# One wide product for the high and low probabilities of attention, and an addition on the way out of PSUM

## The chip, the cores and the metric

The kernel runs on one core of a Trainium2 chip. The metric is the device time of one execution in microseconds. Three runs of the kernel before took 1193.26, 1195.87 and 1196.34 us; the median is 1195.87.

## The reference

Attention with two kinds of masks, and behind it a gated feed-forward layer over all tokens:

```python
# q, k, v: 8 batches, 8 heads, 576 positions, 64 wide, float32
rel = pos[:, None] - pos[None, :]
mask_plain = (rel >= 0) & (rel < 32)                     # heads 0 to 3
mask_dil = (rel >= 0) & (rel < 128) & (rel % 4 == 0)     # heads 4 to 7
scores = np.where(mask, q @ k.T / 8, -1e9)
attn = softmax(scores)                                   # exp(s - max) / (sum + 1e-9)
x = (attn @ v) as 4608 rows of 512
xn = x / sqrt(mean(x * x) + 1e-6) * rms_g
out = (silu(xn @ w_gate) * (xn @ w_val)) @ w_out         # 512 -> 1536 -> 512
```

## The kernel before, in words

**Tiling.** The 4608 rows are cut into 16 units of 288 (u = 0 to 15, half a sequence each). Everything of a unit stands transposed: features on partitions, the 288 rows in the free dimension. The 1536 hidden features are 12 pieces j of 128. Heads go in four pairs c; a pair's attention is cut into blocks: 3 blocks of 96 queries in the plain pairs c = 0 and 1, 4 blocks of 72 queries in the dilated pairs c = 2 and 3 (one for each residue class). So a unit has 14 blocks, 6 of nq = 96 and 8 of nq = 72.

**Precision.** Units 0 and 1 of the attention and unit 0 of the feed-forward layer (NNAT = 2) multiply in float32. All others split each operand in a high part, rounded to a shorter float (F32R), and a low part, the rest, and take three products: high by high, high by low and low by high (`three`, L543 to L545; L407 to L409 for the outputs of attention).

**Slots.** Python writes the order of all instructions out by hand, in slots. Three slots make one piece j: `gate` (12 products of 288 columns into PSUM tile g), `val` (12 into v) and `proj` of the piece before (12 into four tiles acc). A unit of the feed-forward layer is a stage of 36 slots. Behind the 12 products of a slot stand what the attention of the next unit has for it: at most one block's transposes (t, L394, into the free columns of g or v), one block's output products (o, L407 to L409, into the only tile o) and one block's score products (q, L420, into the only tile s). In a stage these blocks come every other slot; a block's outputs come 3 slots after its transposes and share their slot with the scores of a later block. The last about 9 slots of a stage have no outputs.

**What follows a product** on the other engines is put off to the start of the next slot (`later(1, rank, ...)`, `flush`), in the order of the ranks: 0 tanh of g (ACT) or the product with v (DVE, `prod`, L595); 0.2 `untranspose` (ACT copies the transposed probabilities as `pt`, L374, DVE takes the low part `pl`, L378); 0.5 `hhi` (ACT, L606, it waits for `prod`), then `take` (the block's outputs out of PSUM into `xraw`, L347); 0.7 `scores_max` (DVE, L307 and L312); 0.8 silu (DVE, L582). Exponentials, splits of q and k (L276, L281, L285, L290) and of the values (`vhi`, `vlo`, L247, L251) stand in later ranks. Each engine works its instructions off in that order. ACT is ScalarE, DVE VectorE, POOL GpSimd.

`pl` stands in the path of TensorE in one way that matters here: it reads the transposes out of the free columns of g or v, and the next `gate` or `val` starts that tile anew.

Of the kernel before, what the change touches and what calls it, by code (L numbers as in the profile page):

```python
# [9 lines left out]
F32 = mybir.dt.float32  # L10
BF16 = mybir.dt.bfloat16
F32R = mybir.dt.float32r
U32 = mybir.dt.uint32
AF = mybir.ActivationFunctionType
ALU = mybir.AluOpType
PSUM = bass.MemoryType.PSUM

B, H, S, D = 8, 8, 576, 64
DM, FF = 512, 1536
NT = B * S  # L20
P = 128
# [4 lines left out]
QB = 96  # L26
NC = DM // P
NJ = FF // P
NNAT = 2
# [15 lines left out]
def geometry(u, c):  # L45


    half = u % 2
    if c < NC // 2:
        if half:  # L50
            return [(QB * i, QB * i, 0, P) for i in range(U // QB)], QB, U + W
        return [(QB * i, max(QB * i - W, 0), 0 if i else W, P if i else QB)
                for i in range(U // QB)], QB, U
    nq = U // DIL
    keys = nq + (W if half else 0)
    return [(nq * r, keys * r, 0 if half else W, keys) for r in range(DIL)], nq, keys * DIL
# [3 lines left out]
def attn_moe(ctx: ExitStack, tc: tile.TileContext, qk_in, v_in, w_gate, w_val, w_out, rms_g, outT):  # L60
# [4 lines left out]
    V, A, G, PE = nc.vector, nc.scalar, nc.gpsimd, nc.tensor  # L65

    cst = ctx.enter_context(tc.tile_pool(name="cst", bufs=1))
    sb = ctx.enter_context(tc.tile_pool(name="sb", bufs=2))
# [29 lines left out]
    def later(dt, rank, fn):  # L98
        put_off.setdefault(now[0] + dt, []).append((rank, fn))
# [90 lines left out]
    heads, vs, late = {}, {}, []  # L190
# [32 lines left out]
    def load_v(b):  # L223

        if b is not None and b[0] >= NNAT:
            u, c, i = b
            vt = sb.tile([P, 2, D], F32, tag="vt", name=f"vt_{u}_{c}_{i}", bufs=3)
            nc.sync.dma_start(out=vt.rearrange("p a d -> p (a d)"), in_=v_in[u, c][:, i * 2 * D:(i + 1) * 2 * D])
            vs[b] = vt

    def further(b, n):

        k = everything.index(b) + n
        return everything[k] if k < len(everything) else None
# [6 lines left out]
    def split_v(b, dt):  # L241
        k = everything.index(b) % 2

        def hi():
            if k not in vparts:
                vparts[k] = [late[0].tile([P, 2, D], F32R, name=f"v{p}_{k}", bufs=1) for p in ("hi", "lo")]
            A.copy(out=vparts[k][0], in_=vs[b])  # L247

        def lo():
            vh, vl = vparts[k]  # L250
            G.tensor_tensor(out=vl, in0=vs.pop(b), in1=vh, op=ALU.subtract)  # L251
            load_v(further(b, 3))

        later(dt, 3.3, hi)
        later(dt, 5.1, lo)
# [42 lines left out]
    st, xraw, xsq = {}, {}, {}  # L298
# [18 lines left out]
    def scores_exp(u, c, i):  # L317
        blocks, nq, _ = geometry(u, c)
        n = blocks[i][3]
        t, sm = st[u, c, i]  # L320
        for a in range(2):
            A.activation(out=t[:nq, a, :n], in_=t[:nq, a, :n], func=AF.Exp, scale=-1.0,  # L322
                         bias=sm[:nq, a:a + 1], accum_out=sm[:nq, 2 + a:3 + a])
# [11 lines left out]
    def take(u, c, i, o):  # L335

        blocks, nq, _ = geometry(u, c)
        if (u, c) not in xraw:
            xraw[u, c] = sb.tile([P, U], F32, tag="xraw", name=f"xraw_{u}_{c}", bufs=NC)
        x = xraw[u, c]  # L340
        if c < NC // 2:
            to = x[:, QB * i:QB * i + nq]
        else:
            to = x.rearrange("p (j r) -> p r j", r=DIL)[:, i, :]
        copy = V.tensor_copy if i % 2 and u != 1 else A.copy
        for a in range(2):
            copy(out=to[a * D:(a + 1) * D], in_=o[a * D:(a + 1) * D, a * nq:(a + 1) * nq])  # L347
        if i == len(blocks) - 1:
            later(1, 2.5, lambda: square(u, c))

    def square(u, c):
        first = c == 0
        sq = sb.tile([P, U], F32, tag="xsq" if first else "tmp", name=f"sq_{u}_{c}", bufs=1 if first else 2)
        x = xraw[u, c]
        A.activation(out=sq, in_=x, func=AF.Square)
        if u == 0:
            G.tensor_scalar(out=x, in0=x, scalar1=gs[:, c:c + 1], scalar2=1.0, op0=ALU.mult, op1=ALU.mult)
        if first:
            xsq[u] = sq
        else:  # L360
            later(1, 0.4, lambda: (V if c == NC - 1 else G).tensor_tensor(out=xsq[u], in0=xsq[u], in1=sq, op=ALU.add))
# [6 lines left out]
    def untranspose(b, t_ps):  # L368
        blocks, nq, _ = geometry(*b[:2])
        n = blocks[b[2]][3]  # L370
        t_in = t_ps[:n].rearrange("k (a q) -> k a q", a=2)[:, :, :nq]
        exact = b[0] < NNAT
        pt = sb.tile([P, 2, QB], F32 if exact else F32R, tag="pt", name=f"pt_{b[0]}_{b[1]}_{b[2]}", bufs=2)
        A.copy(out=pt[:n, :, :nq], in_=t_in)  # L374
        st[b] = pt
        if not exact:
            pl = late[0].tile([P, 2, QB], F32R, tag="pl", name=f"pl_{b[0]}_{b[1]}_{b[2]}", bufs=2)
            V.tensor_tensor(out=pl[:n, :, :nq], in0=t_in, in1=pt[:n, :, :nq], op=ALU.subtract)  # L378
            st[b] = pt, pl

    def products(q, t, o, t_ps, s_tag="s", o_tag="o"):


        if q:
            s_ps = ps.tile([P, 512], F32, tag=s_tag, name=f"s_{q[0]}_{q[1]}_{q[2]}")
        if o:
            o_ps = ps.tile([P, 512], F32, tag=o_tag, name=f"o_{o[0]}_{o[1]}_{o[2]}")
            pt = st.pop(o)
        if t:
            p, _ = st.pop(t)  # L390
        def transposed(a):
            blocks, nq, _ = geometry(*t[:2])
            n = blocks[t[2]][3]
            PE.transpose(t_ps[:n, a * QB:a * QB + nq], p[:nq, a, :n], ident[:nq, :nq])  # L394

        def output(a):
            blocks, nq, _ = geometry(*o[:2])
            n = blocks[o[2]][3]
            if a:
                return  # L400
            out = o_ps[:, :2 * nq].rearrange("d (a q) -> d a q", a=2)
            if o[0] < NNAT:
                PE.matmul(out, vs.pop(o)[:n].rearrange("k a d -> k (a d)"), pt[:n, :, :nq], start=True, stop=True)
                return
            vh, vl = (part[:n].rearrange("k a d -> k (a d)") for part in vparts[everything.index(o) % 2])
            ph, pl = (part[:n, :, :nq] for part in pt)
            PE.matmul(out, vh, ph, start=True, stop=False)  # L407
            PE.matmul(out, vh, pl, start=False, stop=False)  # L408
            PE.matmul(out, vl, ph, start=False, stop=True)  # L409

        def scored(a):
            blocks, nq, _ = geometry(*q[:2])
            qc, kc, _, n = blocks[q[2]]
            sv = s_ps[:QB].rearrange("q (a t k) -> q a t k", a=2, t=2)
            if q[0] < NNAT:
                qr, kr = heads[q[0], 2 * q[1] + a]
                PE.matmul(sv[:nq, a, 0, :n], qr[:, qc:qc + nq], kr[:, kc:kc + n], start=True, stop=True)
                return
            qs, ks = heads[q[0], 2 * q[1] + a]
            PE.matmul(sv[:nq, a, :, :n], qs[:, qc:qc + nq], ks[:, :, kc:kc + n], start=True, stop=True)  # L420

        parts = [(b, fn, a) for b, fn in ((t, transposed), (o, output), (q, scored)) for a in range(2)]
        for b, fn, a in parts:
            if b:
                fn(a)
        if t:
            later(1, 0.2, lambda: untranspose(t, t_ps))
        if o:
            later(1, 0.5, lambda: take(*o, o_ps))
            if o[0] < NNAT:  # L430
                later(1, 9, lambda: load_v(further(o, 3)))
            far = further(o, 2)
            if far and far[0] >= NNAT:
                split_v(far, 8 if o[0] < NNAT else 1)
        if q:
            later(1, 0.7, lambda: scores_max(*q, s_ps))
            later(2, 2, lambda: scores_exp(*q))
            later(3 if q[0] < NNAT else 4, -1, lambda: scores_norm(*q))
            u, c, i = q
            nxt = after(u, 2 * c, 2)  # L440
            nb = len(geometry(u, c)[0])
            if u < NNAT:
                if u == NNAT - 1 and c == NC - 1 and i == nb - 1:
                    for a in range(2):
                        later(1, 9, lambda a=a: load(NNAT, a))
                        later(5 + a, 9, lambda a=a: split(NNAT, a, (1, 2, 2, 3), G, V))
            elif nxt and i == 0:
                split(*nxt, (1, 2, 2, 3), G, V)
                split(nxt[0], nxt[1] + 1, (2, 3, 3, 4), G, V)
# [224 lines left out]
    for n in range(ends):  # L674
# [8 lines left out]
        if n == ends - 1:  # L683
            _, v_free = gate(0, 0), val(0, 0)
# [3 lines left out]
    for u in range(NU):  # L688
        for j in range(NJ):
            for part in range(0 if u + j else 2, 3):  # L690
                t = 3 * (u * NJ + j) + part
# [94 lines left out]
```

## Time and profile before

| | |
|---|---|
| runs | 1193.26, 1195.87, 1196.34 us |
| profiled execution, its own time | 1192.86 us |
| its span, first to last instruction | 1190.7 us |
| granted TensorE clock over the span | 0.997 |
| TensorE busy with matmuls | 96% |
| VectorE, ScalarE, GpSimd busy | 63%, 57%, 54% |

Busy time is the union of an engine's instructions in the profile; the time of the profiled execution lies 2.2 us above its span, and 3.0 us below the median of the three runs. Starts in the timeline are in us from the start of the span. A matmul's recorded length (about 0.3 us) includes its way through the array and overlaps the next one, so what a product takes of TensorE is read from start to start.

### The profile page before, as it was taken

What the parts mean: (1) busy time and instruction counts of PE and PEld (TensorE: products, weight loads), DVE (VectorE), ACT (ScalarE), POOL (GpSimd) and SP (SyncE); (2) the same over time, 40 slices, a digit from 0 to 9 for tenths busy, and PEclk for the clock granted to TensorE, in tenths of its full rate; (3) what the DMA queues carried; (4) which work ended last, traced back from release to release, by engine and by line L of the source; (5) the groups of instructions that cost most, each with busy time, mean ns of one, the idle gap of its engine ahead of it and who ended that gap; (6) DMA issues with size and microseconds to landing.
All of it is one profiled execution on the core that took longest, in us unless ns stands there. A gap on an engine that the chain in (4) does not pass through costs nothing.

```text
span 1190.7 us, 26009 instructions
## 1 busy us (share of the span) xinstructions
PE 1140.4 (96%) x8492; PEld 1103.2 (93%) x8492; DVE 755.1 (63%) x2715; ACT 676.4 (57%) x2456; POOL 640.8 (54%) x1094
## 2 busy tenths in 40 slices
PE   4788899999999999999999999999999999999998
PEld 3566688999999999999999999999999999999998
DVE  4789786765658576665857656585765757575321
ACT  4567576564646556474656646465665646565221
POOL 2666476664646555464655655465555645565211
PEclk9999899999999999999999999999999999999999
DMA  4555321121213112121312212131221213120000
GB/s 151 188 186 188 106 82 50 58 80 32 77 38 92 45 51 80 35 81 36 90 40 70 68 30 78 38 101 38 68 61 35 81 37 93 40 77 16 1 21 20
DMA packets 62711, 82.19 MB, mean 69 GB/s; under 512 B 7442, under 2 KB 43282, under 8 KB 62578
## 3 DMA queue, kind: packets, MB, share of 16 engines
q1 hardware_dynamic: 61242, 79.60, 21.9%
q8 instruction: 68, 1.11, 0.4%
q10 hardware_dynamic: 1336, 0.94, 0.3%
q14 instruction: 65, 0.53, 0.1%
HBM read 71.08 MB, written 9.44 MB: 68 GB/s over the span
## 4 chain that ended last, share of the span: by engine, by line
PE 78%; DVE 14%; DMA 2%; ACT 2%; issue 2%; POOL 1%; SPq 0%; POOLq 0%; DVEq 0%
PE acc L543 8%; PE acc L544 7%; PE acc L545 7%; PE v L543 7%; PE g L543 7%; PE v L544 7%; PE v L545 7%; PE g L544 7%; PE g L545 7%; PE s L420 3%; DVE qs L290 3%; PE g L394 2%; PE o L408 2%; PE o L409 2%; DVE xraw L514 2%
## 5 line engine op out<-in xcount | busy, mean ns | idle before, releaser
L607 POOL TENSOR_TENSOR hlo<-th,hhi 128x288 fp32r<-128x288 f32 x180 | 145.4, 808 | 218.3 <-ACT hhi L606 214.2
L332 POOL TENSOR_SCALAR t<-t,sm 96x128 f32<-96x128 f32 (+3 forms) x448 | 185.2, 425 | 99.4 <-DVE sm L330 74.1
L543 PE MATMUL v<-xhi,hi_v 128*128 128x288 f32 x720 | 220.3, 306 | 3.5 <-DVE pl L378 3.2
L543 PE MATMUL acc<-hhi,hi_o 128*128 128x288 f32 x720 | 221.1, 307 | 0.0
L543 PE MATMUL g<-xhi,hi_g 128*128 128x288 f32 x720 | 219.8, 305 | 0.0
L544 PE MATMUL acc<-hlo,hi_o 128*128 128x288 f32 x720 | 212.8, 295 | 0.2 <-POOL hlo L607 0.2
L544 PE MATMUL g<-xlo,hi_g 128*128 128x288 f32 x720 | 212.9, 296 | 0.0
L544 PE MATMUL v<-xlo,hi_v 128*128 128x288 f32 x720 | 212.8, 296 | 0.0
L545 PE MATMUL acc<-hhi,lo_o 128*128 128x288 f32 x720 | 212.6, 295 | 0.0
L545 PE MATMUL g<-xhi,lo_g 128*128 128x288 f32 x720 | 212.6, 295 | 0.0
L545 PE MATMUL v<-xhi,lo_v 128*128 128x288 f32 x720 | 212.3, 295 | 0.0
L322 ACT ACTIVATE t<-t,sm 96x128 f32<-96x128 f32 (+3 forms) x448 | 166.7, 375 | 18.4 <-DMA k<-in_qk_dram 13.6
L251 POOL TENSOR_TENSOR vlo<-vt,vhi 128x128 fp32r<-128x128 f32 x196 | 98.5, 502 | 125.2 <-ACT vhi L247 109.3
L577 ACT ACTIVATE th<-g 128x288 f32<-128x288 f32 x180 | 74.0, 411 | 157.7 <-PE g L545 106.2
L606 ACT CAST hhi<-th 128x288 fp32r<-128x288 f32 x180 | 78.0, 433 | 141.2 <-DVE th L595 137.2
L543 PEld LDWEIGHTS v<-xhi,hi_v 128*128 128x128 f32 x720 | 135.3, 188 | 6.5 <-DVE pl L378 6.5
L307 DVE TENSOR_TENSOR t<-s,mask 96x256 f32<-96x256 f32 (+3 forms) x196 | 72.0, 367 | 106.7 <-PE s L420 101.1
L544 PEld LDWEIGHTS acc<-hlo,hi_o 128*128 128x128 f32 x720 | 135.8, 189 | 0.5 <-POOL hlo L607 0.5
L544 PEld LDWEIGHTS g<-xlo,hi_g 128*128 128x128 f32 x720 | 135.7, 188 | 0.1
L544 PEld LDWEIGHTS v<-xlo,hi_v 128*128 128x128 f32 x720 | 135.7, 188 | 0.0
L543 PEld LDWEIGHTS acc<-hhi,hi_o 128*128 128x128 f32 x720 | 135.5, 188 | 0.0
L543 PEld LDWEIGHTS g<-xhi,hi_g 128*128 128x128 f32 x720 | 135.3, 188 | 0.2 <-issue 0.2
(120 smaller groups left out, 2662.0 us busy)
## 6 DMA issues: line engine op xcount, KB each, us to landing
qk<-in_qk_dram SPq DMA_DIRECT2D x56, 288.0 KB, 2.9
vt<-in_v_dram SPq DMA_DIRECT2D x196, 64.0 KB, 1.8
qk<-in_qk_dram SPq DMA_DIRECT2D x28, 352.0 KB
out_dram<-ot SPq DMA_DIRECT2D x64, 144.0 KB, 1.9
qk<-in_qk_dram SPq DMA_DIRECT2D x28, 304.0 KB, 2.7
raw_g<-in_w_gate_dram SPq DMA_DIRECT2D x12, 512.0 KB, 3.1
raw_v<-in_w_val_dram SPq DMA_DIRECT2D x12, 512.0 KB, 4.0
raw_o<-in_w_out_dram SPq DMA_DIRECT2D x12, 512.0 KB
```

What stands on the lines that cost most here:

```text
L251: G.tensor_tensor(out=vl, in0=vs.pop(b), in1=vh, op=ALU.subtract)
L290: eq.tensor_tensor(out=qs[D:], in0=qr[D:], in1=qs[D:], op=ALU.subtract)
L307: V.tensor_tensor(out=t[:nq, :, :n], in0=sv[:nq, :, 1, :n], in1=mask[:nq, None, mc:mc + n].to_broadcast([nq, 2, n]), op=ALU.add)
L322: A.activation(out=t[:nq, a, :n], in_=t[:nq, a, :n], func=AF.Exp, scale=-1.0, bias=sm[:nq, a:a + 1], accum_out=sm[:nq, 2 + a:3 + a])
L332: G.tensor_scalar(out=t[:nq, a, :n], in0=t[:nq, a, :n], scalar1=sm[:nq, 2 + a:3 + a], scalar2=1.0, op0=ALU.mult, op1=ALU.mult)
L420: PE.matmul(sv[:nq, a, :, :n], qs[:, qc:qc + nq], ks[:, :, kc:kc + n], start=True, stop=True)
L543: PE.matmul(out, wh[:, cc, :], xh, start=start, stop=False)
L544: PE.matmul(out, wh[:, cc, :], xl, start=False, stop=False)
L545: PE.matmul(out, wl[:, cc, :], xh, start=False, stop=stop)
L577: A.activation(out=t, in_=g, func=AF.Tanh, scale=0.5)
L606: A.copy(out=hi, in_=t)
L607: G.tensor_tensor(out=lo, in0=t, in1=hi, op=ALU.subtract)
```

## The change

For the units from 2 on, the low part of the probabilities is no longer a tile of its own: `pt` gets a second half for it. The high part of the values is multiplied with both halves in one product of 4 nq columns, whose left half (2 nq columns) is high by high and whose right half is high by low. The third product, low values by high probabilities, is accumulated on the left half. So two products stand where three stood. The right half is added on the way out: `take` copies it to `xraw` on ACT (two instructions, one for each head of the pair), and then DVE adds the left half (two instructions). Before, `take` was two copies for each block, on DVE for odd i (block number in the pair) and on ACT for even i.

```diff
@@ take
-        for a in range(2):
-            copy(out=to[a * D:(a + 1) * D], in_=o[a * D:(a + 1) * D, a * nq:(a + 1) * nq])
+        if u < NNAT:
+            for a in range(2):
+                copy(out=to[a * D:(a + 1) * D], in_=o[a * D:(a + 1) * D, a * nq:(a + 1) * nq])
+        else:
+            for a in range(2):
+                A.copy(out=to[a * D:(a + 1) * D], in_=o[a * D:(a + 1) * D, (2 + a) * nq:(3 + a) * nq])
+            for a in range(2):
+                rows = slice(a * D, (a + 1) * D)
+                V.tensor_tensor(out=to[rows], in0=o[rows, a * nq:(a + 1) * nq], in1=to[rows], op=ALU.add)
@@ untranspose
-        pt = sb.tile([P, 2, QB], F32 if exact else F32R, tag="pt", ...)
-        A.copy(out=pt[:n, :, :nq], in_=t_in)
-        st[b] = pt
+        st[b] = pt = sb.tile([P, 2, 2, QB], F32 if exact else F32R, tag="pt", ...)
+        A.copy(out=pt[:n, 0, :, :nq], in_=t_in)
         if not exact:
-            pl = late[0].tile([P, 2, QB], F32R, tag="pl", ...)
-            V.tensor_tensor(out=pl[:n, :, :nq], in0=t_in, in1=pt[:n, :, :nq], op=ALU.subtract)
-            st[b] = pt, pl
+            V.tensor_tensor(out=pt[:n, 1, :, :nq], in0=t_in, in1=pt[:n, 0, :, :nq], op=ALU.subtract)
@@ products, output
-            ph, pl = (part[:n, :, :nq] for part in pt)
-            PE.matmul(out, vh, ph, start=True, stop=False)
-            PE.matmul(out, vh, pl, start=False, stop=False)
-            PE.matmul(out, vl, ph, start=False, stop=True)
+            both = o_ps[:, :4 * nq].rearrange("d (t a q) -> d t a q", t=2, a=2)
+            PE.matmul(both, vh, pt[:n, :, :, :nq], start=True, stop=False)
+            PE.matmul(out, vl, pt[:n, 0, :, :nq], start=False, stop=True)
```

In the changed kernel the lines stand elsewhere: L347 becomes L351 (ACT) and L354 (DVE), L378 becomes L383, L407 to L409 become L412 and L413, L420 becomes L424, L595 becomes L599, L606 becomes L610, L543 becomes L547.

**TensorE, at the end of a `val` slot**, with the outputs of block i = 1 of pair 0 and the scores of a later block. Names are tile, pair or head or piece, block, and a running number; the sizes are those of what is read and streamed. Before:

```order
L545 MATMUL v_0_7198<-xhi_3_7119,lo_v_674 128x288
L407 MATMUL o_0_1_7212<-pt_0_1_7111,vhi_1468 128x192
L408 MATMUL o_0_1_7212<-pl_0_1_7113,vhi_1468 128x192
L409 MATMUL o_0_1_7212<-pt_0_1_7111,vlo_1469 128x192
L420 MATMUL s_1_2_7211<-ks_2_6901,qs_2_6936 96x256
L420 MATMUL s_1_2_7211<-ks_3_6934,qs_3_6968 96x256
```

and now:

```order
L549 MATMUL v_0_7196<-xhi_3_7117,lo_v_674 128x288
L412 MATMUL o_0_1_7210<-pt_0_1_7110,vhi_1468 128x384
L413 MATMUL o_0_1_7210<-pt_0_1_7110,vlo_1469 128x192
L424 MATMUL s_1_2_7209<-ks_2_6901,qs_2_6936 96x256
L424 MATMUL s_1_2_7209<-ks_3_6934,qs_3_6968 96x256
```

One product is gone and one is twice as wide; no other row moves.

**VectorE in the slot after that**, from the product with v to the low part of the next transposes. Before:

```order
L595 TENSOR_TENSOR th_0_7186<-th_0_7186,v_0_7198 128x288 [waits DVE_49,PE_49]
L347 COPY xraw_0_7149<-o_0_1_7212 64x96 [waits PE_49]
L347 COPY xraw_0_7149<-o_0_1_7212 64x96
L307 TENSOR_TENSOR t_1_2_7225<-s_1_2_7211,mask 96x256 [waits PE_49]
L312 ISA t_1_2_7225,sm_1_2_7227<-s_1_2_7211,t_1_2_7225 96x128 [waits DVE_49]
L312 ISA sm_1_2_7227 96x1
L312 ISA t_1_2_7225,sm_1_2_7227<-s_1_2_7211,t_1_2_7225 96x128
L312 ISA sm_1_2_7227 96x1
L329 TENSOR_SCALAR sm_1_1_7154<-sm_1_1_7154 96x2 [waits Activation_49]
L330 RECIPROCAL sm_1_1_7154<-sm_1_1_7154 96x2 [waits DVE_49]
L378 TENSOR_TENSOR pl_1_0_7254<-v_0_7198,pt_1_0_7252 128x192 [waits Activation_49]
```

and now:

```order
L599 TENSOR_TENSOR th_0_7185<-th_0_7185,v_0_7196 128x288 [waits DVE_49,PE_49]
L354 TENSOR_TENSOR xraw_0_7146<-o_0_1_7210,xraw_0_7146 64x96 [waits PE_49,Activation_49]
L354 TENSOR_TENSOR xraw_0_7146<-o_0_1_7210,xraw_0_7146 64x96
L307 TENSOR_TENSOR t_1_2_7224<-s_1_2_7209,mask 96x256 [waits PE_49]
L312 ISA t_1_2_7224,sm_1_2_7226<-s_1_2_7209,t_1_2_7224 96x128 [waits DVE_49]
L312 ISA sm_1_2_7226 96x1
L312 ISA t_1_2_7224,sm_1_2_7226<-s_1_2_7209,t_1_2_7224 96x128
L312 ISA sm_1_2_7226 96x1
L329 TENSOR_SCALAR sm_1_1_7153<-sm_1_1_7153 96x2
L330 RECIPROCAL sm_1_1_7153<-sm_1_1_7153 96x2 [waits DVE_49]
L383 TENSOR_TENSOR pt_1_0_7251<-v_0_7196,pt_1_0_7251 128x192 [waits Activation_49]
```

The additions stand where the copies stood, and the first of them waits for ACT. The first addition waits for both copies of ACT: they give one signal, after the second.

**ScalarE in the same slot.** Before:

```order
L374 CAST pt_0_2_7188<-g_0_7167 128x192
L322 ACTIVATE t_1_1_7152,sm_1_1_7154<-t_1_1_7152,sm_1_1_7154 96x128 [waits DVE_49] x2
L606 CAST hhi_0_7219<-th_0_7186 128x288 [waits DVE_49]
L247 CAST vhi_1468<-vt_1_0_6816 128x128 [waits DMAHW6_49,PE_49]
L374 CAST pt_1_0_7252<-v_0_7198 128x192 [waits PE_49]
```

and now:

```order
L322 ACTIVATE t_1_1_7151,sm_1_1_7153<-t_1_1_7151,sm_1_1_7153 96x128 [waits DVE_49] x2
L610 CAST hhi_0_7216<-th_0_7185 128x288 [waits DVE_49]
L351 COPY xraw_0_7146<-o_0_1_7210 64x96 [waits PE_49]
L351 COPY xraw_0_7146<-o_0_1_7210 64x96
L247 CAST vhi_1468<-vt_1_0_6815 128x128 [waits DMAHW6_49]
L381 CAST pt_1_0_7251<-v_0_7196 128x192 [waits PE_49]
```

ACT's copies of the block stand behind `hhi`, which waits for `prod` on DVE. For even i they stood at this place of their slots before; there DVE now has the additions ahead of the scores.

More of the change, by code (lines that the diff above doesn't have):

```diff
@@ L372, in untranspose @@
         exact = b[0] < NNAT
-        pt = sb.tile([P, 2, QB], F32 if exact else F32R, tag="pt", name=f"pt_{b[0]}_{b[1]}_{b[2]}", bufs=2)
-        A.copy(out=pt[:n, :, :nq], in_=t_in)
-        st[b] = pt
+        st[b] = pt = sb.tile([P, 2, 2, QB], F32 if exact else F32R, tag="pt", name=f"pt_{b[0]}_{b[1]}_{b[2]}", bufs=2)
+        A.copy(out=pt[:n, 0, :, :nq], in_=t_in)
         if not exact:
-            pl = late[0].tile([P, 2, QB], F32R, tag="pl", name=f"pl_{b[0]}_{b[1]}_{b[2]}", bufs=2)
-            V.tensor_tensor(out=pl[:n, :, :nq], in0=t_in, in1=pt[:n, :, :nq], op=ALU.subtract)
-            st[b] = pt, pl
+            V.tensor_tensor(out=pt[:n, 1, :, :nq], in0=t_in, in1=pt[:n, 0, :, :nq], op=ALU.subtract)
     def products(q, t, o, t_ps, s_tag="s", o_tag="o"):
@@ L402, in output @@
             if o[0] < NNAT:
-                PE.matmul(out, vs.pop(o)[:n].rearrange("k a d -> k (a d)"), pt[:n, :, :nq], start=True, stop=True)
+                PE.matmul(out, vs.pop(o)[:n].rearrange("k a d -> k (a d)"), pt[:n, 0, :, :nq], start=True, stop=True)
                 return
             vh, vl = (part[:n].rearrange("k a d -> k (a d)") for part in vparts[everything.index(o) % 2])
-            ph, pl = (part[:n, :, :nq] for part in pt)
-            PE.matmul(out, vh, ph, start=True, stop=False)
-            PE.matmul(out, vh, pl, start=False, stop=False)
-            PE.matmul(out, vl, ph, start=False, stop=True)
+            both = o_ps[:, :4 * nq].rearrange("d (t a q) -> d t a q", t=2, a=2)
+            PE.matmul(both, vh, pt[:n, :, :, :nq], start=True, stop=False)
+            PE.matmul(out, vl, pt[:n, 0, :, :nq], start=False, stop=True)
         def scored(a):
```

## The prediction

> **What bounds the kernel now.** I read the first page first: engines, slices, clock.
>
> ```profile
> span 1190.7 us, 26009 instructions
> PE 1140.4 (96%) x8492; PEld 1103.2 (93%) x8492; DVE 755.1 (63%) x2715; ACT 676.4 (57%) x2456; POOL 640.8 (54%) x1094
> PE   4788899999999999999999999999999999999998
> ```
>
> TensorE (PE) is the bound from the sixth slice on; it idles noticeably only in the first 150 us, where the change does nothing (units 0 and 1 keep the old path). Then the list of waits, for what still stops PE in the steady part, and the sums by stretch for the load of the others.
>
> ```profile
> PE v L543 <- DVE pl L378: 3.2, 13, 0.7
> 505.00:553.00 48.00, 47.74 (x379) 47.29 (x378) 32.44 (x126) 30.40 (x118) 28.97 (x53) 1.00 0.23 70
> 509.00:513.00 4.00, 4.00 (x34) 4.00 (x33) 3.80 (x12) 2.46 (x10) 2.22 (x4) 1.00 0.39 108
> ```
>
> The columns of a stretch are its length, busy time of PE, weight loads, DVE, ACT and POOL, then the granted clock (full), DMA share and GB/s. The one wait by which another engine holds up products in the steady part is that of `val` for `pl` (13 times, about once a stage). In the 48 us of a stage that hold nearly all its outputs DVE is busy 32.4 us, but in 509 to 513 it is busy 3.80 of 4: on average there is room, in places none. So the change has two sides: what it takes off PE, and what it puts into the queues of DVE and ACT ahead of `pl`.
>
> **Part 1: two products for three.** From start to start, in the timeline of PE:
>
> ```profile
> 508.31 0.29 PE L543 MATMUL g<-xhi,hi_g 128*128 128x288 f32 x1
> 508.71 0.30 PE L543 MATMUL g<-xhi,hi_g 128*128 128x288 f32 x1
> ...
> 511.30 0.25 PE L407 MATMUL o<-pt,vhi 128*128 128x192 f32 x1
> 511.38 0.28 PE L408 MATMUL o<-pl,vhi 128*128 128x192 f32 x1
> 511.50 0.28 PE L409 MATMUL o<-pt,vlo 128*128 128x192 f32 x1
> 511.61 0.40 PE L420 MATMUL s<-ks,qs 128*96 128x256 f32 x2
> ...
> 530.90 0.23 PE L407 MATMUL o<-pt,vhi 104*128 104x144 f32 x1
> 530.97 0.28 PE L408 MATMUL o<-pl,vhi 104*128 104x144 f32 x1
> 531.08 0.27 PE L409 MATMUL o<-pt,vlo 104*128 104x144 f32 x1
> 531.20 0.36 PE L420 MATMUL s<-ks,qs 128*72 128x208 f32 x2
> ```
>
> Between the two L543 rows lie three products of 288 columns in 0.40 us: 0.133 each, 0.46 ns a column. Three output products take 0.31 us at nq = 96 and 0.30 at nq = 72, though these stream a quarter fewer columns: the steps behind L408 and L409 are 0.11 to 0.12 for 192 columns as for 144. I read that as the load of the next 128 weight columns, which a short product does not cover. The new first product streams 384 or 288 columns (0.177 or 0.133) and covers it. By 0.46 ns a column the pair takes 0.266 or 0.200, a saving of 0.045 or 0.10 us. A stage has 6 blocks of the one and 8 of the other, 6 x 0.045 + 8 x 0.10 = 1.07 us; 14 stages hold such attention (units 2 to 15), so PE gets 15 us back. From below: if the wide product ran at three times the old step with its own load bare, nothing is gained; from above: the whole third step goes, 0.11 x 196 = 21.6 us. I take the 15, since 288 columns is the shape of most products here.
>
> The Trainium skill, "TensorE: Matmul & The Clock Gate", section "Back-to-back issue gap", gives N/2.4 + 2.5 ns for an isolated warm product; by that alone the columns stay the same and only one 2.5 ns goes for each block, 0.5 us in all. The rows above speak against it here (0.11 for 144 columns, where that formula gives an estimate of 0.06), and the same section says that weight loads and products set the spacing together.
>
> **Part 2: `pt` in one tile.** ACT and DVE do the same instructions into another address. The first product now needs `pl` itself; `pl` is made two slots earlier, so that costs nothing while `pl` is less than a slot late.
>
> **Part 3: `take`.** Costs by form:
>
> ```profile
> L347 ACT COPY xraw<-o 64x72 f32<-64x72 f32 x136 | 38.2, 281 | 17.1 <-PE o L409 14.8
> L347 DVE COPY xraw<-o 64x72 f32<-64x72 f32 x120 | 34.0, 284 | 37.2 <-PE o L409 34.9 <-PE o L403 1.5
> L347 DVE COPY xraw<-o 64x96 f32<-64x96 f32 x60 | 15.1, 252 | 0.4
> L378 DVE TENSOR_TENSOR pl<-g,pt 128x192 fp32r<-128x192 f32 x55 | 19.6, 357 | 11.9 <-ACT pt L374 9.3
> L378 DVE TENSOR_TENSOR pl<-g,pt 104x144 fp32r<-104x144 f32 x35 | 10.8, 308 | 14.8 <-ACT pt L374 14.2
> ```
>
> No row shows an addition of this size. `pl` also reads PSUM and SBUF on DVE; from 144 to 192 columns it grows by 49 ns, 1.0 ns a column, which carried down gives 0.26 us at 96 columns and 0.23 at 72. The strided copy of 72 takes longer (284) than the plain one of 96 (252), so 0.23 to 0.29 for the strided addition; I take 0.26 for all, two to a block. Even blocks (8 of 14) put 0.52 us on DVE that was not there; odd blocks swap two copies for two additions, about even, and give ACT two copies more (0.5 us). A stage gains 4.2 us on DVE and 3 on ACT. By sums both have room. The order matters more: DVE now stands still ahead of `scores_max` until ACT has copied, and in the slot after `val` ACT copies only after `hhi`, which waits for DVE's `prod`. Behind a blocked addition stand `scores_max` (the next scores need its tile s), silu (the next `gate` needs g), the norm of the softmax (POOL scales by it, then come the transposes) and `pl`; `pl` is needed soonest, one slot after its transposes. Three places in a stage have a `pl` out of v right behind that slot, with the next `val` one slot off.
>
> Place 1:
>
> ```profile
> 508.19 0.42 DVE L307 TENSOR_TENSOR t<-s,mask 96x256 f32<-96x256 f32 x1 [0.33 <-PE s L420]
> 509.18 1.00 DVE L290 TENSOR_TENSOR qs<-qk,qs 64x288 fp32r<-64x288 f32 x1
> 511.39 0.53 DVE L290 TENSOR_TENSOR qs<-qk,qs 64x288 fp32r<-64x288 f32 x1
> 511.95 0.46 DVE L595 TENSOR_TENSOR th<-th,v 128x288 f32<-128x288 f32 x1
> 512.32 0.52 DVE L347 COPY xraw<-o 64x96 f32<-64x96 f32 x2
> 512.87 0.42 DVE L307 TENSOR_TENSOR t<-s,mask 96x256 f32<-96x256 f32 x1
> 514.17 0.36 DVE L378 TENSOR_TENSOR pl<-v,pt 128x192 fp32r<-128x192 f32 x1
> 514.45 0.81 DVE L631 TENSOR_SCALAR ot<-acc 128x288 f32<-128x288 f32 x2
> ...
> 508.37 0.48 ACT L347 COPY xraw<-o 64x96 f32<-64x96 f32 x2
> 512.44 0.43 ACT L606 CAST hhi<-th 128x288 fp32r<-128x288 f32 x1 [1.11 <-DVE th L595]
> ...
> 515.73 0.31 PE L543 MATMUL v<-xhi,hi_v 128*128 128x288 f32 x1
> ```
>
> ACT's copies end at 508.85, the additions at 509.4; the scores that began at 508.19 begin 1.2 late. L290 of 1.00 us is late by then and likely as short as its second of 0.53; `prod` starts at about 512.45 instead of 511.95. Then `hhi` (0.4), copies (0.5) and additions (0.5), so the scores start at 514.35 instead of 512.87; from there to `pl` it is 1.30 as before and `pl` ends at 516.0. `val` would start at 515.73 less three savings of 0.045, 515.6: PE waits 0.4 to 0.5 us, where before `pl` was 1.2 early.
>
> Place 2, two pieces on:
>
> ```profile
> 517.54 0.46 DVE L595 TENSOR_TENSOR th<-th,v 128x288 f32<-128x288 f32 x1
> 518.03 0.43 ACT L606 CAST hhi<-th 128x288 fp32r<-128x288 f32 x1
> 520.21 0.47 ACT L347 COPY xraw<-o 64x96 f32<-64x96 f32 x2
> 523.62 0.45 DVE L595 TENSOR_TENSOR th<-th,v 128x288 f32<-128x288 f32 x1
> 525.85 0.31 DVE L378 TENSOR_TENSOR pl<-v,pt 104x144 fp32r<-104x144 f32 x1 [0.17 <-ACT pt L374]
> 527.48 0.31 PE L543 MATMUL v<-xhi,hi_v 128*128 128x288 f32 x1
> ```
>
> After place 1 DVE still has L631 (0.8), additions (0.5), scores, silu and the norm ahead of `prod`: 518.9 instead of 517.5. `hhi` and all behind it on ACT come 1.4 late, so the copies of 520.21 come at 521.6, DVE's additions end at 522.7, and its next `prod` starts at 525.5 instead of 523.6. Again `hhi`, copies, additions (1.4 us), scores, norm and `pl` (1.5): 528.9, against a `val` due at 527.5 plus the 0.3 that PE is late by then: a wait of about 1.2. Place 3, in the dilated pairs:
>
> ```profile
> 538.36 0.28 DVE L378 TENSOR_TENSOR pl<-v,pt 104x144 fp32r<-104x144 f32 x1
> 539.16 0.31 PE L543 MATMUL v<-xhi,hi_v 128*128 128x288 f32 x1
> ```
>
> `pl` was 0.52 early there; `hhi`, copies and additions put it back by 1.0: a wait of about 0.5. Later places have fewer scores and wait little. Each wait gives DVE time to catch up, and the nine slots without outputs clear the rest.
>
> **The sum.** 0.45 + 1.2 + 0.5 = 2.15 us of waits in a stage, less 1.07 saved: 1.1 us a stage, 15 us over 14 stages. The profiled execution took 1192.86 us, so 1208; the median of the runs stands 3.0 above that execution, so 1211. Bounds of the waits: 1.2 us a stage (0.4 at each place) if nothing is passed on from one place to the next, +2 us in all; and 3.5 if at each place L290 stays at 1.0, 0.45 more, +34.
>
> **Rivals.**
> Queues keep up: DVE takes the additions without a wait that reaches PE, as its 32.4 us in 48 and the 1.2 us that `pl` is early at place 1 allow if additions are short and ACT's copies come at once. Then all of part 1 stays: 1195.9 - 15 = 1181. The point from which it decides is at place 1: a delay of `pl` under 1.1 us. Against it: `hhi` and copies alone are 0.9 on top of what the slot before is late.
> Break-even: waits of about 1.0 us a stage cancel the saving; 1193 to 1199.
> The pair is no cheaper: if streaming alone set the pace, or the four short runs of 72 columns in one product streamed slower than 288 in a row, PE gains nothing and the waits of 2.15 x 14 = 30 us stay: about 1226. Against it: the score row at 531.20, two products of two runs of 104 columns each, ends 0.36 us after its start, no longer for its columns than the row at 511.61 (0.40 for 256); four runs are not shown. The formula of the Trainium skill quoted above would give this outcome too.
>
> **Chances.** Waits outrun the saving, 1200 to 1224: 0.55. Queues keep up, 1178 to 1192: 0.22. Break-even: 0.13. No cheaper pair, 1218 to 1235: 0.10. The predicted time is that of the likeliest, 1211. The range reaches from 1186 to 1230, which leaves out about half of the keep-up case and the far end of the last. A measurement of this kernel can tell about 0.3% (3.6 us) from no change: faster 0.22, same 0.13, slower 0.65.
>
> **What would show it.** Right: starts from the wide product to L424 of 0.27 and 0.20 us; PE waits of `val` (L547) on DVE `pt` L383, several a stage and 20 to 40 us in all, where `pl` had 3.2; DVE waiting on ACT `xraw` L351 ahead of L354; `hhi` (L610) later after its `val`. Wrong: PE without such waits and stages of 68 us (keeps up), or a pair that still takes 0.30 us. What would break the sum is mostly the length of an addition and whether ACT has copied by the time DVE arrives.

## The result, and the profile after

The changed kernel took 1235.55 us (median of 5 runs, 1233.51 to 1238.58); the kernel before, run beside it, 1194.30 (5 runs, 1193.26 to 1196.34). The ratio is 1.0345, 95% interval 1.0325 to 1.0366: slower by 41 us. The forecast was 1211 with 1186 to 1230: the side was right, and the time lies 5.5 us above the upper end.

The first page of the profile after, engines and span:

```profile
span 1233.7 us, 26093 instructions
PE 1142.2 (93%) x8296; PEld 1088.7 (88%) x8296; DVE 789.1 (64%) x2939; ACT 719.3 (58%) x2624; POOL 631.9 (51%) x1094
```

There are 196 products fewer, one for each block, and the span is 43 us longer: TensorE (PE) now stops. DVE is busy 34 us longer (789.1 against 755.1) at 64% of the span: by sums it has as much room as before. Where PE stops stands in the list of waits (us in total, times, longest); rows of after first, then those of before:

```profile
DVE xraw L354 <- ACT xraw L351: 221.8, 179, 2.7
PE g L398 <- DVE sm L329: 32.9, 46, 1.0
PE g L398 <- DVE th L586: 8.9, 16, 1.9
PE v L547 <- DVE pt L383: 3.3, 13, 0.7
```

```profile
PE g L394 <- DVE sm L329: 1.9, 7, 0.3
PE g L394 <- DVE th L582: 0.8, 1, 0.8
```

`val`'s wait for the low part, on which the forecast put 20 to 40 us, reads 3.3 us, as before (3.2). The new wait is another one: the *transposes* (L398; L394 before) that go into the free columns of g at the end of a `val` slot. They had 2.7 us of waits, and now have 41.8. Silu (L586) reads g, so the transposes may write into g only behind it. The profile names L329 in most rows because that is the small instruction that ended last on DVE behind silu; a run below settles that it is silu.

A list of waits counts idle time only. Read from start to start a stop costs a little more, so I also went through PE's starts from 220 us to the last `val`: each product is allowed 0.46 ns a column (or about 0.11 us where the next weight load is longer), and what it comes later than that is put down to the stop in front of it. I call that lateness; the table of the runs below uses it. Before it is 12.2 us in all, after 65.0: 50.0 at those transposes (5.1 before), 11.9 at `val` for the low part (5.9), 3.6 at score products and at the `val` right behind a late one. So 52.8 us more of stops, 15 us less of products: 38 of the 43 us by which the spans differ; the other 5 lie outside that stretch or below what the method resolves.

**One place.** The slot of place 1 of the forecast, in the timeline of the kernel after (here and below, rows between those shown are left out):

```profile
530.28 0.34 PE L412 MATMUL o<-pt,vhi 128*128 128x384 f32 x1
530.46 0.25 PE L413 MATMUL o<-pt,vlo 128*128 128x192 f32 x1
530.66 0.38 PE L424 MATMUL s<-ks,qs 128*72 128x208 f32 x2
531.10 0.40 PE L547 MATMUL v<-xhi,hi_v 128*128 128x288 f32 x1
532.67 0.29 PE L549 MATMUL v<-xhi,lo_v 128*128 128x288 f32 x1
533.84 0.36 PE L398 MATMUL g<-ident,t 96*128 96x96 f32 x2 [0.88 <-DVE sm L329]
```

```profile
527.67 0.45 DVE L599 TENSOR_TENSOR th<-th,v 128x288 f32<-128x288 f32 x1
529.00 0.52 DVE L354 TENSOR_TENSOR xraw<-o,xraw 64x96 f32<-64x96 f32 x2 [0.88 <-ACT xraw L351]
529.55 0.42 DVE L307 TENSOR_TENSOR t<-s,mask 96x256 f32<-96x256 f32 x1
530.71 0.33 DVE L383 TENSOR_TENSOR pt<-v,pt 128x192 fp32r<-128x192 f32 x1
530.97 0.81 DVE L635 TENSOR_SCALAR ot<-acc 128x288 f32<-128x288 f32 x2
531.91 0.52 DVE L354 TENSOR_TENSOR xraw<-o,xraw 64x96 f32<-64x96 f32 x2
532.47 0.37 DVE L307 TENSOR_TENSOR t<-s,mask 72x208 f32<-72x208 f32 x1
533.25 0.44 DVE L586 SCALAR_TENSOR_TENSOR th<-th,g 128x288 f32<-128x288 f32 x1
```

and on ACT:

```profile
528.15 0.43 ACT L610 CAST hhi<-th 128x288 fp32r<-128x288 f32 x1 [1.77 <-DVE th L599]
528.50 0.47 ACT L351 COPY xraw<-o 64x96 f32<-64x96 f32 x2
```

The same place before:

```profile
515.54 0.35 PE L420 MATMUL s<-ks,qs 128*72 128x208 f32 x2
517.21 0.29 PE L545 MATMUL v<-xhi,lo_v 128*128 128x288 f32 x1
517.37 0.36 PE L394 MATMUL g<-ident,t 96*128 96x96 f32 x2
```

```profile
516.00 0.37 DVE L307 TENSOR_TENSOR t<-s,mask 72x208 f32<-72x208 f32 x1 [0.74 <-PE s L420]
516.78 0.45 DVE L582 SCALAR_TENSOR_TENSOR th<-th,g 128x288 f32<-128x288 f32 x1
```

Before, DVE waited 0.74 us for the scores, silu ended at 517.23, and the transposes came at 517.37, hardly late (0.16 us behind the product before them, where 0.13 is the usual step). After, DVE loses 0.88 us waiting for ACT, which copies behind `hhi`, and from 529.00 on works with hardly a pause; silu ends at 533.69 and the transposes come at 533.84. From the start of the scores to the transposes it took 1.83 us before and takes 3.18 now, 1.35 more. `val` starts 0.44 behind the scores instead of 0.19, which makes 0.25 of that; the other 1.10 is the stop of the transposes. By start-to-start lateness this stop is 1.06 us, 0.88 of it idle; the next such places in this stage have 1.10, 1.00 and 0.57.

The 0.14 or 0.15 us from the end of silu to the transposes are no slack. A `val` slot ends in such transposes 65 times from 220 us on, five times a stage. In the kernel after, all 65 start 0.145 to 0.147 us behind the recorded end of silu, however long the stop: so long the signal from DVE to TensorE takes here. In the kernel before, 34 of the 65 stood at that distance already, and the farthest stood 0.39 behind.

The same over the whole run, in the groups by line: what DVE's first instruction on the scores (L307) found when it got there, before and after. Behind the bar stand busy us, mean ns, and the idle time ahead of it with what ended it:

```profile
L307 DVE TENSOR_TENSOR t<-s,mask 96x256 f32<-96x256 f32 (+3 forms) x196 | 72.0, 367 | 106.7 <-PE s L420 101.1 <-POOL t L332 2.5
```

```profile
L307 DVE TENSOR_TENSOR t<-s,mask 96x256 f32<-96x256 f32 (+3 forms) x196 | 71.9, 367 | 17.6 <-PE s L424 12.1
```

Before, DVE was ahead and waited 101 us for scores; after, 12: the time that it had in hand there now goes to waiting for ACT, and silu comes behind.

### The profile page after: what moved, and what is told of

Its sections match the earlier page's. It is cut to its first block, busy times and chain, and to the rows that moved or that the text cites. A ratio compares the mean times of both kernels' runs of the same rounds, so it can differ in the third digit from the quotient of the medians.

```text
span 1233.7 us, 26093 instructions
## 1 busy us (share of the span) xinstructions
PE 1142.2 (93%) x8296; PEld 1088.7 (88%) x8296; DVE 789.1 (64%) x2939; ACT 719.3 (58%) x2624; POOL 631.9 (51%) x1094
## 4 chain that ended last, share of the span: by engine, by line
PE 48%; DVE 29%; ACT 12%; issue 5%; DMA 3%; POOL 2%; POOLq 0%; ACTq 0%; SPq 0%; DVEq 0%
PE acc L547 5%; PE acc L548 5%; PE acc L549 5%; DVE qs L290 5%; PE g L547 4%; PE g L549 4%; PE g L548 4%; DVE t L312 4%; DVE t L307 4%; PE v L547 4%; PE v L548 3%; ACT t L322 3%; PE v L549 3%; ACT xraw L351 3%; DVE xraw L354 3%
## 5 line engine op out<-in xcount | busy, mean ns | idle before, releaser
L354 DVE TENSOR_TENSOR xraw<-o,xraw 64x96 f32<-64x96 f32 (+1 forms) x392 | 107.1, 273 | 226.2 <-ACT xraw L351 221.8
L547 PE MATMUL v<-xhi,hi_v 128*128 128x288 f32 x720 | 223.1, 310 | 4.7 <-DVE pt L383 3.3
L547 PE MATMUL acc<-hhi,hi_o 128*128 128x288 f32 x720 | 221.0, 307 | 0.0
L547 PE MATMUL g<-xhi,hi_g 128*128 128x288 f32 x720 | 219.9, 305 | 0.0
L610 ACT CAST hhi<-th 128x288 fp32r<-128x288 f32 x180 | 78.0, 434 | 152.9 <-DVE th L599 150.7
L547 PEld LDWEIGHTS v<-xhi,hi_v 128*128 128x128 f32 x720 | 135.2, 188 | 12.8 <-DVE pt L383 10.8
L251 POOL TENSOR_TENSOR vlo<-vt,vhi 128x128 fp32r<-128x128 f32 x196 | 90.9, 464 | 103.4 <-ACT vhi L247 74.6
L549 PEld LDWEIGHTS acc<-hhi,lo_o 128*128 128x128 f32 x720 | 135.4, 188 | 0.0
L547 PEld LDWEIGHTS g<-xhi,hi_g 128*128 128x128 f32 x720 | 135.2, 188 | 0.2 <-issue 0.2
```

Source lines behind the costliest of these rows:

```text
L354: V.tensor_tensor(out=to[rows], in0=o[rows, a * nq:(a + 1) * nq], in1=to[rows], op=ALU.add)
L547: PE.matmul(out, wh[:, cc, :], xh, start=start, stop=False)
L549: PE.matmul(out, wl[:, cc, :], xh, start=False, stop=stop)
L610: A.copy(out=hi, in_=t)
```

## The experiments

| run | what differs from the kernel after | us, median | ratio to before [95%] | lateness: transposes into g | val for low part | scores | all |
|---|---|---|---|---|---|---|---|
| before | | 1194.30 | 1 | 5.1 | 5.9 | 0 | 12.2 |
| after | | 1235.55 | 1.0345 [1.0325, 1.0366] | 50.0 | 11.9 | 3.6 | 65.0 |
| product_only | right half left out, old copies | 1178.18 | 0.9879 [0.9852, 0.9906] | 5.1 | 6.1 | 0 | 11.6 |
| take_only | three products, same take | 1243.34 | 1.0425 [1.0398, 1.0453] | 49.4 | 8.4 | 1.1 | 58.9 |
| no_act_wait | copies to two tiles, no sum | 1229.88 | 1.0311 [1.0288, 1.0334] | 47.0 | 12.1 | 2.9 | 61.4 |
| silu_first | silu ahead of take | 1197.17 | 1.0035 [1.0021, 1.0049] | 0 | 9.1 | 13.7 | 26.1 |
| dve_length | all copies on DVE, no wait for ACT | 1191.71 | 0.9990 [0.9974, 1.0005] | 18.8 | 6.0 | 0 | 24.3 |
| wait_alone | all copies on ACT, DVE only waits | 1197.48 | 1.0035 [1.0017, 1.0053] | 25.7 | 6.3 | 0 | 31.5 |
| add_later | additions behind scores and silu | 1183.46 | 0.9924 [0.9909, 0.9939] | 5.3 | 6.0 | 0 | 12.3 |
| before_silu_first | kernel before, silu early | 1186.34 | 0.9951 [0.9935, 0.9968] | 0 | 6.0 | 0 | 6.0 |
| add_later_silu_first | both moves | 1176.73 | 0.9852 [0.9831, 0.9873] | 0 | 5.9 | 1.3 | 7.3 |
| product_only_silu_first | product_only, silu early | 1172.55 | 0.9820 [0.9805, 0.9835] | 0 | 6.0 | 0 | 5.4 |

Each ratio is to the kernel before on the same chip (1192.84 to 1194.30 there). Lateness is in us as explained above, good to 1 or 2 us; "scores" are the stops at and around the score and output products, and small rest items are in "all" alone. Where `val` stops for the low part right behind a late score product, that stop is under "scores" too: about two thirds of the 3.6 of after, and over half of the 13.7 of silu_first.

**product_only: the wide product without what it costs on the way out.** The take is that of the kernel before; the right half is left out of the result.

```diff
-            for a in range(2):
-                A.copy(out=to[...], in_=o[..., (2 + a) * nq:(3 + a) * nq])
-            for a in range(2):
-                V.tensor_tensor(out=to[rows], in0=o[rows, ...], in1=to[rows], op=ALU.add)
+            for a in range(2):
+                copy(out=to[...], in_=o[..., a * nq:(a + 1) * nq])
```

> The wide product alone: two products as in the changed kernel, but take copies only the left half, on ACT or DVE by turns as before (the right half, high values by low probabilities, is left out of the output). Theory (the products are cheaper as costed, all loss comes from the way out of PSUM): DVE and ACT do what they did before, the streaming saving of 13 us stays whole, 1194 - 13 = 1181 us, no transposes waiting for silu beyond the few of before. Rival (the wide product or the larger tile pt itself delays something): 1190 us or more.

Measured 1178.18 us (1176.03 to 1181.25), 14.9 below the 1193.09 of before, and lateness as before (11.6 against 12.2). The saving on PE is there when nothing more waits (by the interval of the ratio 11 to 18 us, with 15 forecast). This excludes the rival of a pair that is no cheaper.

**take_only: the new take without the cheaper product.** The high by low product goes into the right half by itself, so there are three products again.

```diff
-            PE.matmul(both, vh, pt[:n, :, :, :nq], start=True, stop=False)
-            PE.matmul(out, vl, pt[:n, 0, :, :nq], start=False, stop=True)
+            PE.matmul(both[:, 0], vh, pt[:n, 0, :, :nq], start=True, stop=False)
+            PE.matmul(both[:, 1], vh, pt[:n, 1, :, :nq], start=False, stop=False)
+            PE.matmul(both[:, 0], vl, pt[:n, 0, :, :nq], start=False, stop=True)
```

> The way out of PSUM alone: three products of 2 nq columns as before, the middle one into the right half of o; take copies the right half on ACT and adds the left on DVE. Theory: the waits of the changed kernel (52 us of slips more than before) with no saving, 1240 to 1250 us, slower than the changed kernel. Rival (the loss needs the wide product): under 1215 us.

Measured 1243.34 us (1242.76 to 1244.51): the take alone costs 50 us. Between this run and the kernel after only the products differ, and the ratios differ by 0.8%, 9.5 us, of the 15 that the products save. The rest went into longer stops (58.9 us of lateness here, 65.0 there): that fits a PE that comes earlier to a point that DVE opens, and so waits longer at it.

**silu_first: only silu moved**, ahead of take and scores on DVE (not in the first piece of unit 0, where tanh comes late). L329 and all else keep their places.

```diff
-        later(1, 0.8, silu)
+        later(1, 0.45 if u + j else 0.8, silu)
```

> The changed kernel with silu at rank 0.45, ahead of the additions and scores_max in DVE's queue, all else the same. Theory (the transposes at the end of a val slot wait until silu has read g; 50 of 65 us of slips): those waits go, the val waits for the low part stay or grow a little (12 to 25 us), 1190 to 1205 us. Rival (DVE is short of time as such, and the stall only moves to another tile): 1220 us or more.

Measured 1197.17 us (1194.23 to 1201.01). The rows of its list of waits that answer to those of after:

```profile
DVE xraw L354 <- ACT xraw L351: 166.4, 133, 2.4
PE v L547 <- DVE pt L383: 4.0, 16, 0.7
PE v L398 <- DVE th L599: 3.8, 10, 1.6
PE g L398 <- DVE th L586: 0.9, 1, 0.9
```

The row of L398 behind L329 is gone, with L329 where it was: the transposes waited for silu (they start 0.58 us or more behind its end now). (Those into v wait a little for `prod` now, L599, 2.6 us of lateness.) One number in the order of DVE is worth 38 us; the additions and DVE's wait for ACT (166 us) are still there. But scores and maxima are now later still. Some 6 us of lateness stand at score products, which wait until DVE has read the scores before out of s: one starts 0.29 us late at 516.61, 0.15 behind the end of DVE's last reading (L312). Right behind it `val` is another 0.32 late (its first two products, at 517.05 and 517.29): it starts 0.06 behind the end of the low part (L383).

**no_act_wait: a miss.** ACT copies the right half to a tile that nothing reads, and DVE copies the left half; the sum is left out. No data passes from ACT to DVE.

```diff
-                A.copy(out=to[...], in_=o[..., (2 + a) * nq:(3 + a) * nq])
+                A.copy(out=side[..., :nq], in_=o[..., (2 + a) * nq:(3 + a) * nq])
-                V.tensor_tensor(out=to[rows], in0=o[rows, ...], in1=to[rows], op=ALU.add)
+                V.tensor_copy(out=to[rows], in_=o[rows, ...])
```

> The changed kernel, but ACT copies the right half into a spare tile that nobody reads, and DVE copies the left half to xraw instead of adding (the sum of the halves is left out). DVE has as many instructions of nearly the same length (copies of 252 and 284 ns for additions of 255 and 287), only its wait for ACT is gone. Theory (the wait for ACT, 222 us in all, holds back scores, silu and then the transposes): 1181 to 1200 us. Rival (the length of the two more DVE instructions does it): 1220 us or more.

Measured 1229.88 us (1229.19 to 1230.86). The edit did not take the wait away:

```profile
DVE xraw L355 <- ACT side L352: 210.3, 167, 2.6
PE g L399 <- DVE sm L329: 31.8, 46, 0.9
```

DVE's copy still waits for a semaphore of ACT; the one tile that both touch is o in PSUM. So the run tells nothing on a kernel without the wait, though its time lies in the range of the rival; it only shows that it makes little difference (5.7 us, the intervals overlap) whether DVE copies or adds there.

**dve_length and wait_alone: the two costs apart.** In dve_length (right half left out) DVE copies every block and ACT none: DVE's extra length in even blocks, without the wait. In wait_alone (right half left out) ACT copies every block and DVE reads one column of o into an unread tile, which waits for ACT as the additions do but takes 0.16 us.

```diff
 dve_length
+        copy = V.tensor_copy if u >= NNAT or (i % 2 and u != 1) else A.copy
 wait_alone
+        copy = V.tensor_copy if u == 0 and i % 2 else A.copy
+        if u >= NNAT:
+            V.tensor_copy(out=side, in_=o[:, :1])
```

> The wide product with the left half alone copied out, by DVE for every block (no copies on ACT; the right half is left out of the output). DVE has the instructions of the changed kernel in number, place and about length (copies of 252 and 284 ns), and no wait for ACT. Theory W (what holds back silu is that DVE waits until ACT has read the tile o): near the product alone, 1178 to 1192 us. Theory L (two more DVE instructions ahead of scores and silu are enough): 1205 to 1232 us.

> The wide product with the left half alone copied out, by ACT for every block (the right half is left out), and one DVE copy of a single column of o into a tile that nobody reads, at the place of the additions: it shares no data with ACT's copies, only the tile o in PSUM. DVE has 0.2 us a block less to do than in the changed kernel's additions by about 0.4 us, but it waits for ACT. Theory W: 1205 to 1230 us. Theory L: 1178 to 1192 us.

Measured 1191.71 (1188.80 to 1196.30) and 1197.48 us (1194.17 to 1197.85): 13.5 and 19.3 us above product_only. Waits of wait_alone, then of dve_length (the transposes are L394 and L391 there):

```profile
DVE side L350 <- ACT xraw L347: 245.8, 192, 3.0
PE g L394 <- DVE sm L329: 15.7, 46, 0.6
```

```profile
PE g L391 <- DVE sm L329: 7.3, 28, 0.5
```

Neither is the cause alone: dve_length stands at the upper end of what W gives for it, and wait_alone between the ranges of W and L. Apart they cost 33 us, together (after against product_only) 57. That fits the place shown above, where DVE's 0.74 us of waiting for scores swallow the first 0.7 us of a delay; what comes on top counts in full. That this is why they come to more than their sum is worked out from that place, not tested by itself.

**add_later: the additions behind the scores and silu.** ACT's copies stay; DVE's additions go to rank 0.9.

```diff
 take
-            for a in range(2):
-                V.tensor_tensor(out=to[rows], in0=o[rows, ...], in1=to[rows], op=ALU.add)
 after the output products
+            if o[0] >= NNAT:
+                later(1, 0.9, lambda: join(*o, o_ps))      # the same two additions
```

> The changed kernel with DVE's additions at rank 0.9, behind scores_max and silu of the same slot; ACT's copies stay at 0.5. Theory (place in DVE's queue, by either W or L): scores and silu stand as before and the additions find ACT's copies done, so the streaming saving comes through with 5 to 15 us of waits beyond the product alone: 1181 to 1195 us. Rival (DVE has no time for the additions): 1210 us or more.

Measured 1183.46 us (1181.56 to 1184.18), 9.4 us faster than before. The same additions, the same lengths; only their place differs (the transposes are L403 here):

```profile
DVE xraw L361 <- ACT xraw L351: 56.7, 52, 1.8
PE g L403 <- DVE sm L329: 1.9, 7, 0.3
```

ACT has mostly copied by the time DVE arrives (56.7 us of waits for 221.8), and the transposes' row is that of the kernel before. The run stands 5 us above product_only; where these lie is told with the floor below.

**before_silu_first: the same move of silu in the kernel before.**

> The kernel before with silu at rank 0.45. Control for the run with silu first: if silu first helps by itself, this shows how much. In the kernel before the transposes wait 5 us in all for silu: 1188 to 1195 us against 1193, so at most a third of a per cent; by the rival (silu first gains 38 us whatever stands ahead of it) 1160 us.

Measured 1186.34 us (1185.28 to 1187.26), 6.5 below before and a little below the range: the edge between silu and the transposes was already at its limit, and its lateness of 5 us goes to 0.

**Both moves, and their floor.** add_later_silu_first has the additions at 0.9 and silu at 0.45; product_only_silu_first is product_only (right half left out) with silu at 0.45.

> The additions behind the scores (rank 0.9) and silu ahead of take and scores (0.45 for all pieces but the first of unit 0). Theory (only what stands ahead of silu, the scores and the low part of pt on DVE costs PE time; what is left with the additions late is 6 us of transposes waiting for silu and 6 us of val waiting for the low part): silu early takes the 6 us away as it did in the kernel before, so 1183.5 - 6 = 1177 us, and the slips of PE between 220 us and the end fall from 12 to about 6 us. Rival (early silu pushes the maxima of the scores back by 0.45 us and the score products then wait for the only tile s, as with silu alone moved, where that cost 11 us): no gain or a loss over the late additions alone, 1183 to 1190 us, with waits of L424-like score products on DVE.

> The wide product, the right half left out of the result, the copies as before by turns on ACT and DVE, and silu at 0.45. This is the floor that the additions can be measured against. Theory: the transposes' waits for silu (5 us in the run with the wide product alone) go, 1178.2 - 5 = 1173 us; the distance from it to the run with late additions and early silu is what the additions still cost, expected within 5 us. Rival: the waits for silu were not what stopped PE there, and it stays at 1178.

Measured 1176.73 (1175.11 to 1178.44) and 1172.55 us (1171.46 to 1173.31). From the list of waits of the first:

```profile
PE v L554 <- DVE pt L388: 3.7, 15, 0.7
PE o L417 <- DVE xraw L361: 1.3, 2, 1.0
PE g L403 <- DVE th L593: 0.9, 1, 0.9
```

The rival's stops of score products stayed away but for 1.3 us of lateness at score and output products. The first of the two computes all that the kernel before computes and is 16.9 us (1.5%) faster than it, the fastest such version here. The additions still cost 4 us against the floor, and by the profiles most of that stands in one stage: from the first copy of unit 0's outputs (`ot`) to the first of unit 1's it takes 79.6 us against 76.1, from there to unit 15's 930.2 against 929.0. Likewise add_later against product_only, 80.7 and 76.8, then 935.1 and 934.7. In the seven runs in which ACT copies every block that stage takes 79.5 to 81.7 us, in the five others 76.1 to 77.9. So the rest goes with ACT's copies or with DVE's waiting for them; which of the two no run separates.

## Why the prediction was right on the side and wrong on the size

**Products: right.** Forecast from start to start: 0.177 and 0.133 us for the wide product, 0.266 and 0.200 for the pair. Measured in the plain pairs, at 526.38, 526.55 and 526.64: 0.17 and 0.09, 0.26 together; in the dilated pairs:

```profile
548.72 0.30 PE L412 MATMUL o<-pt,vhi 104*128 104x288 f32 x1
548.85 0.23 PE L413 MATMUL o<-pt,vlo 104*128 104x144 f32 x1
548.92 0.36 PE L424 MATMUL s<-ks,qs 128*72 128x208 f32 x2
```

0.13 and 0.07, 0.20 together. The medians over all blocks from 220 us on are 0.26 and 0.20, where three products took 0.31 and 0.29: about 15 us over the run, and product_only came out 14.9 faster. That the step of 0.11 is a weight load was read from the rows, not tested: the step behind L409 is 0.11 too, though the load there has only 96 or 72 columns. The formula in the Trainium skill's page "TensorE: Matmul & The Clock Gate", section "Back-to-back issue gap", would have kept the columns the only price (an estimate of 0.5 us of saving); the runs go against that here.

**Additions: right.** Forecast 0.26, 0.23 to 0.29. Groups by line, with mean ns of one behind the busy us, and the idle time before them:

```profile
L354 DVE TENSOR_TENSOR xraw<-o,xraw 64x72 f32<-64x72 f32 x224 | 64.2, 287 | 142.9 <-ACT xraw L351 141.4
L354 DVE TENSOR_TENSOR xraw<-o,xraw 64x96 f32<-64x96 f32 x168 | 42.8, 255 | 83.4 <-ACT xraw L351 80.4
```

DVE's wait for ACT, named in the forecast, is the largest new wait in the profile.

**`val` for the low part: right at place 1, too much behind it.** Forecast 0.45, 1.2 and 0.5 us at the three places of a stage; lateness in the stage from 531 us 0.45, 0.40 and 0.17 (0.11 and 0.13 of the first two are the score products'). The forecast passed DVE's delay on from place 1 to place 2. The transposes stopped in between (1.06, 1.10 and 1.00 us) and gave DVE that time; in silu_first, where they don't stop, 0.53 us appear near place 2, half at the score products and half at `val`. Over the whole run the term was some +8 us, not +30: +6 in its column of the table, and what stands under "scores".

**The step that failed** is the list of what stands behind a blocked addition: "silu (the next `gate` needs g)" and "`pl` is needed soonest". Both are wrong. Tile g has two users: the next `gate`, a slot and more away, and the transposes of the next block, which write into its free columns at the end of the same `val` slot. By the timeline of before that use came 0.14 us behind silu, which is all taken by the signal, while `pl` was 1.2 us early at place 1. The tightest edge was left out of the sum, and it cost 45 us more than before (50.0 of lateness against 5.1). The signs stood in the profile of before: waits of 1.9 and 0.8 us at L394, small but of exactly that pair, where the prediction calls `val`'s wait for `pl` the only one in the steady part. The errors went both ways: 45 us left out there, some 22 too much for `val` (30 against 8), 1 left out at score products. That makes, within what the count resolves, the 25 us between the forecast and 1235.55.

**Rivals.** "Queues keep up" did not hold, though its 1181 us is what the change is worth when the additions stand elsewhere (add_later 1183.46). Its deciding point, less than 1.1 us of delay of `pl` at place 1, was on the wrong instruction. "Break-even" and "no cheaper pair" are excluded by after and product_only. The second came nearest in time (about 1226, 1218 to 1235), but by luck: the pair is as cheap as forecast, and the time went elsewhere.

## What to carry to other kernels

Before putting an instruction into an in-order queue, list for everything behind it every later user of every tile that it reads or writes, not only the next one that comes to mind, and read each one's slack from start and end times: a tile with free columns lent to another job has two deadlines. Waits of a few tenths in the profile before mark the edges with no slack. They are the ones to look at, though not all of them grow: here, in the lists of waits, the transposes' went from 2.7 to 41.8 us, and that of `val` for the low part from 3.2 to 3.3. Place a step that waits for another engine behind those with a deadline: the same change cost 41 us with the additions at one place in the queue and gained 9 with them at another, with no change in the work.

## What was not expected of the hardware

Two engines that read disjoint halves of one PSUM tile, with no data between them, stood one behind the other all the same: 210.3 us in 167 waits in no_act_wait. The wait is a semaphore in the program (the trace has 191 semaphore instructions of DVE at that line), which the kernel's text does not show. Silu and the transposes are such a pair too: silu reads the first 288 columns of g, and the transposes write the columns behind them. The Trainium skill, "PSUM — Partial Sum Buffer", section "PSUM bank collisions raise a hardware error", gives a reason: two engines must not touch the same bank and the same quadrant of partitions at once, ScalarE's and VectorE's reads included and disjoint columns too, and software has to keep them apart. The wait of ACT and DVE seen here agrees; no run here lets them collide. So in this kernel, adding the two halves of one tile on the way out through two engines took the sum of both their times, not the longer of them.
